# The first matrix product of the second part by one level of Strassen's scheme: seven half-size products instead of eight, 768 tokens at a time

## The chip, the core and the metric

The kernel runs on one core of a Trainium2 chip. The metric is device time in microseconds (us) of one execution, the median of several runs. The engines of the core run side by side, each in its own order: TensorE (PE in the profile, with its weight loads as PEld), VectorE (DVE), ScalarE (ACT), GpSimd (POOL), and SyncE (SP), which here issues DMA transfers. They share the on-chip memory SBUF; PE writes its results into the banks of a second memory, PSUM, from which DVE and ACT read.

## What is computed

```python
def phi(x):
    proj = np.einsum('bhsd,df->bhsf', x, w_phi)
    proj = proj - np.max(np.abs(proj), axis=-1, keepdims=True)
    return np.concatenate([np.exp(proj), np.exp(-proj)], axis=-1)
q_p, k_p = (phi(q), phi(k))
kv = np.einsum('bhsf,bhsd->bhfd', k_p, v)
z = np.sum(k_p, axis=2)
num = np.einsum('bhsf,bhfd->bhsd', q_p, kv)
den = np.einsum('bhsf,bhf->bhs', q_p, z)[..., None] + 1e-06
x = (num / den).transpose(0, 2, 1, 3).reshape(4608, 512)
...
h = x @ w_in
g = h - np.tanh(h)
return (g @ w_out).astype(np.float32)
```

Batch 8, 8 heads, 576 positions, head size 64. The second part takes 4,608 tokens of 512 numbers through w_in (512 x 2048), the function h - tanh(h), and w_out (2048 x 512). The weights of the second part arrive as 64-bit floats.

## The kernel before

**The first part** (`ramp`, `period`, `drain`) runs over 32 units, each a pair of heads of one batch entry, and writes the normalised result of each to `xs` in device memory. Beside it, each period decodes one 128 x 512 tile of w_in or w_out from 64-bit floats (`dec_0` to `dec_3`), and from the fifth period on `split_w` splits one into a high and a low half for the reduced-precision matmul type fp32r: a copy on ACT (`wh`), then the difference `w - wh` on POOL (L96). All of this stands in an order written by hand.

**The second part** runs over nine groups `g` of 512 tokens and, in each, over 16 tiles `f` of 128 columns of w_in: 144 steps. `stage1` (L617) multiplies the tile with the group's tokens: 12 matmuls (four slices of the 512-long contraction, each as high x high, high x low, low x high) of 512 columns into one PSUM bank `ph`. Then ACT and DVE form h - tanh(h): a polynomial for small |h| and the direct difference for the rest, chosen by a mask. ACT makes `y`, `s1`, `s2`, `th`, `mk` (L632 to L640); DVE makes five steps:

```python
nc.vector.scalar_tensor_tensor(s1, s1, PC1, y, ALU.add, ALU.mult)
gs = s2 if g else s1
nc.vector.scalar_tensor_tensor(gs, s2, PC2, s1, ALU.add, ALU.mult)
nc.vector.scalar_tensor_tensor(gs, gs, PA, h, ALU.mult, ALU.mult)
hh = th if g else h
nc.vector.tensor_tensor(hh, h, th, ALU.subtract)
nc.vector.copy_predicated(gs, mk.bitcast(U32), hh)
```

(L641, L643, L644, L646, L647). Here `h` lies in PSUM, so L644 and L646 read one operand from SBUF and one from PSUM; `s1`, `s2`, `y`, `mk`, `th` lie in SBUF, except that in the first group `s2` is a PSUM bank, `ex`, and L646 writes back into PSUM. `split_g` splits the result into `gh` (a copy on ACT, L653) and `gl` (a difference on POOL, L654), and `stage2` (L665) runs 12 matmuls of 512 columns, four token tiles by three, into four PSUM banks `po` that gather over the 16 steps. A step's `stage2` is issued two steps after its `stage1`. While a group runs, `x_load` and `x_split` fetch and split the next group's tokens (L117 on ACT, L118 on DVE), and in the first group the 18 weight tiles that the first part left are split (`late`). The scheduler of the framework orders this part, apart from instructions that `pin` keeps in program order.

Of the kernel before, what the change touches and what calls it, by code (L numbers as in the profile page):

```python
# [32 lines left out]
def tile_linear_attention_moe(  # L33
# [44 lines left out]
    wpa = ctx.enter_context(tc.tile_pool(name="wpa", bufs=1, reuse_waits="tile"))
    xp0 = ctx.enter_context(tc.tile_pool(name="xp0", bufs=1, reuse_waits="tile"))
    wi, wo, wp, xp = {}, {}, [], []  # L80


    def split_w(n, pin=lambda ins: ins):
        d, nm, f = (wi, wo)[n % 2], "io"[n % 2], n // 2
        early = f < AHEAD
        w = d[f]
        wh = (wpa if early else wp[0]).tile([P, DM], F32R, name=f"wh{nm}{f}")
        wl = wpool.tile([P, DM], F32R, tag="w", name=f"wl{nm}{f}")
        if early or nm == "i":
            pin(nc.scalar.copy(wh, w))  # L90
        else:
            pin(nc.vector.tensor_copy(wh, w))
        d[f] = (wh, wl)

        def low():
            pin(nc.gpsimd.tensor_tensor(wl, w, f32(wh), ALU.subtract))  # L96
# [18 lines left out]
    def x_split(xt, c, order=lambda ins: ins):
        xh, xl = (x[:, c, :] for x in xt)
        order(nc.scalar.copy(xh, f32(xl)))  # L117
        order(nc.vector.tensor_tensor(xl, f32(xl), f32(xh), ALU.subtract))  # L118

    with ExitStack() as c1:
        raw = c1.enter_context(tc.tile_pool(name="raw", bufs=2))
        p1 = c1.enter_context(tc.tile_pool(name="p1", bufs=1))
        p2 = c1.enter_context(tc.tile_pool(name="p2", bufs=2))
        dr = ctx.enter_context(tc.tile_pool(name="dr", bufs=3, space=DRAM))
# [94 lines left out]
        def part_of(u, part):  # L223
# [136 lines left out]
        def denom_copy(u):  # L360
            u.dd = p1.tile([P, CH], F32, tag="dd", name=f"dd{u.i}")
# [56 lines left out]

        def ramp():
# [52 lines left out]
        def period(i):  # L472
            a, c, p, r, q, o = (unit(i - n) for n in range(6))
            w = dec[i - 3]
            low = split_w(i - 4) if 4 <= i < 2 * AHEAD + 4 else None
# [43 lines left out]
            if i == NU - 1:  # L519
                for j in range(NCT // 2):  # L520
                    x_split(xt[0], j)
            if i == NU - 2:
                xt[0] = x_tiles(0)
                for j in range(NCT):
                    x_load(0, xt[0], j)
# [13 lines left out]
        def drain():  # L539
# [30 lines left out]
            for j in range(NCT // 2, NCT):  # L570
                x_split(xt[0], j)
# [33 lines left out]
    with ExitStack() as c2:  # L605
        xp.append(c2.enter_context(tc.tile_pool(name="xp", bufs=1, reuse_waits="tile")))
        wp.append(c2.enter_context(tc.tile_pool(name="wp", bufs=1, reuse_waits="tile")))
        gp = c2.enter_context(tc.tile_pool(name="gp", bufs=2, reuse_waits="tile"))
        gm = c2.enter_context(tc.tile_pool(name="gm", bufs=2, reuse_waits="tile"))
        ps_h = c2.enter_context(tc.tile_pool(name="ps_h", bufs=3, reuse_waits="tile", space=PSUM))  # L610
        ps_o = c2.enter_context(tc.tile_pool(name="ps_o", bufs=5, reuse_waits="tile", space=PSUM))

        ex = ps_o.tile([P, DM], F32, tag="o", name="ex")

        def stage1(g, f, xh, xl):  # L617
            n = G
            N = n * P
            ph = ps_h.tile([P, 512], F32, tag="h", name=f"ph{g}_{f}")  # L620
            h = ph[:, 0:N]
            i = 0
            for c in range(NCT):
                for wt, x in ((wi[f][0], xh), (wi[f][0], xl), (wi[f][1], xh)):
                    nc.tensor.matmul(h, wt[:, c * P : (c + 1) * P], x[:, c, 0:N], start=(i == 0), stop=(i == 3 * NCT - 1))  # L625
# [8 lines left out]
            nc.scalar.activation(s1, y, AF.Square, bias=bias_t[:, 0:1])  # L634
            s2 = tmp("s2") if g else ex
            nc.scalar.activation(s2, y, AF.Square, bias=bias_t[:, 1:2])  # L636
            th = tmp("th")
            nc.scalar.activation(th, h, AF.Tanh)
            mk = tmp("o", bufs=3) if (g, f) == steps[-1] else tmp("mk", bufs=1)
            nc.scalar.activation(mk, y, AF.Relu, bias=bias_t[:, 2:3])  # L640
            nc.vector.scalar_tensor_tensor(s1, s1, PC1, y, ALU.add, ALU.mult)  # L641
            gs = s2 if g else s1
            nc.vector.scalar_tensor_tensor(gs, s2, PC2, s1, ALU.add, ALU.mult)  # L643
            nc.vector.scalar_tensor_tensor(gs, gs, PA, h, ALU.mult, ALU.mult)  # L644
            hh = th if g else h
            nc.vector.tensor_tensor(hh, h, th, ALU.subtract)  # L646
            nc.vector.copy_predicated(gs, mk.bitcast(U32), hh)  # L647
            return gs
# [145 lines left out]
```

## Time and profile before

| | us |
|---|---|
| median of 3 runs | 1102.42 (1102.21 to 1102.55) |
| the profiled execution | 1103.19 |
| its span, first to last instruction | 1101.4 |
| first matmul of the second part | 313.15 from the span's start |
| start of the last matmul | 1097.09 |
| DVE busy, 400.20 to 1097.10 | 490.02 of 696.90 |
| ACT busy, the same stretch | 460.96 |
| POOL busy, the same stretch | 170.70 |

The page gives, for each engine, its busy time and its share of the span; then the chain of work that ended last; then groups of instructions by line with their mean duration. A busy share is an average over the two parts, which have different limits, so the second part has its own rows here. The granted TensorE clock is 1.000.

### The profile page before, as it was taken

How to read it: one execution, taken by the hardware profiler on the slowest of the kernel's cores; microseconds unless marked ns; L12 is line 12 of the kernel's file. 1: busy time of each engine (PE TensorE's matmuls, PEld its weight loads, DVE VectorE, ACT ScalarE, POOL GpSimd, SP SyncE). 2: the span in 40 equal slices, each digit the busy share in tenths (PEclk: the TensorE clock that was granted, in tenths of full speed). 3: DMA queues.
4: the chain of work that ended last, by engine and by line, in shares of the span. 5: the costliest groups of instructions: out<-in, count | busy, mean ns of one | idle time of the engine just before them, and what ended most of it. 6: DMA issues, size and time to landing. Idle time of an engine off the chain costs nothing.

```text
span 1101.4 us, 18540 instructions
## 1 busy us (share of the span) xinstructions
PE 1092.3 (99%) x6956; PEld 862.2 (78%) x6956; DVE 838.8 (76%) x1169; ACT 768.9 (70%) x1398; POOL 438.6 (40%) x349
## 2 busy tenths in 40 slices
PE   8999999999999999999999999999999999999998
PEld 6666676766668888888888888888888888888886
DVE  7999999999988777767667667767767676776665
ACT  5888887777877766666667666666666666666665
POOL 4788887666655532322222222222222222222222
PEclk9999999999999999999999999999999999999999
DMA  5677777777630020010011011001002002000001
GB/s 173 185 224 224 221 221 217 216 214 211 210 113 1 1 78 12 33 48 30 1 39 39 1 39 39 1 12 64 1 1 77 1 1 77 1 1 22 17 1 39
DMA packets 51147, 85.46 MB, mean 78 GB/s; under 512 B 13296, under 2 KB 24944, under 8 KB 51056
## 3 DMA queue, kind: packets, MB, share of 16 engines
q1 hardware_dynamic: 36656, 51.89, 14.8%
q10 hardware_dynamic: 14400, 32.38, 9.8%
q8 instruction: 55, 0.90, 0.3%
q14 instruction: 36, 0.29, 0.1%
HBM read 65.08 MB, written 19.02 MB: 76 GB/s over the span
## 4 chain that ended last, share of the span: by engine, by line
PE 98%; ACT 1%; DVE 1%; DMA 0%; POOL 0%; issue 0%; SPq 0%; ACTq 0%; POOLq 0%; DVEq 0%
PE ph L625 35%; PE po L668 12%; PE po L669 12%; PE po L671 12%; PE pc L285 6%; PE po L334 6%; PE pu L348 3%; PE pj L219 3%; PE pa L219 3%; PE ptt L249 2%; PE pc L323 1%; PE pt L219 1%; PE pu L306 1%; PE pu L254 1%; PE pu L315 0%; DMA rb<-rr 0%
## 5 line engine op out<-in xcount | busy, mean ns | idle before, releaser
L654 POOL TENSOR_TENSOR gl<-s,gh 128x512 fp32r<-128x512 f32 x144 | 186.4, 1294 | 551.9 <-ACT gh L653 543.4
L632 ACT ACTIVATE y<-ph 128x512 f32<-128x512 f32 x144 | 86.2, 598 | 252.1 <-PE ph L625 252.1
L641 DVE SCALAR_TENSOR_TENSOR s<-s,y 128x512 f32<-128x512 f32 x144 | 102.2, 710 | 183.8 <-ACT s L634 182.8
L625 PE MATMUL ph<-xh,whi 128*128 128x512 f32 x576 | 224.3, 389 | 0.1
L625 PE MATMUL ph<-xl,whi 128*128 128x512 f32 x576 | 224.1, 389 | 0.0
L625 PE MATMUL ph<-xh,wli 128*128 128x512 f32 x576 | 224.1, 389 | 0.0
L668 PE MATMUL po<-who,gh 128*128 128x512 f32 x572 | 222.6, 389 | 0.0
L669 PE MATMUL po<-wlo,gh 128*128 128x512 f32 x572 | 222.5, 389 | 0.0
L671 PE MATMUL po<-who,gl 128*128 128x512 f32 x572 | 152.9, 389 | 0.0
L647 DVE COPY_PREDICATED s<-mk,th 128x512 f32<-128x512 uint32 x127 | 122.1, 961 | 13.7 <-DVE th L646 0.9
L625 PEld LDWEIGHTS ph<-xh,whi 128*128 128x128 f32 x576 | 108.2, 188 | 23.3 <-DVE s L647 0.5
L625 PEld LDWEIGHTS ph<-xh,wli 128*128 128x128 f32 x576 | 108.2, 188 | 22.5
L625 PEld LDWEIGHTS ph<-xl,whi 128*128 128x128 f32 x576 | 108.0, 188 | 22.3
L668 PEld LDWEIGHTS po<-who,gh 128*128 128x128 f32 x572 | 107.4, 188 | 22.7 <-ACT gh L653 0.4
L669 PEld LDWEIGHTS po<-wlo,gh 128*128 128x128 f32 x572 | 107.4, 188 | 22.2
L671 PEld LDWEIGHTS po<-who,gl 128*128 128x128 f32 x572 | 107.4, 188 | 22.2
L634 ACT ACTIVATE s<-y,bias_t 128x512 f32<-128x512 f32 x144 | 104.4, 725 | 0.4 <-POOL gl L654 0.4
L644 DVE SCALAR_TENSOR_TENSOR s<-s,ph 128x512 f32<-128x512 f32 x144 | 98.9, 687 | 5.2
L640 ACT ACTIVATE mk<-y,bias_t 128x512 f32<-128x512 f32 x143 | 102.8, 719 | 0.0
L643 DVE SCALAR_TENSOR_TENSOR s<-s,s 128x512 f32<-128x512 f32 x128 | 88.5, 692 | 15.0 <-ACT s L636 1.9
L636 ACT ACTIVATE s<-y,bias_t 128x512 f32<-128x512 f32 x128 | 92.4, 722 | 1.6 <-POOL gl L654 1.6
L653 ACT CAST gh<-s 128x512 fp32r<-128x512 f32 x144 | 88.8, 617 | 2.4 <-DVE s L647 2.4
(103 smaller groups left out, 1695.6 us busy)
## 6 DMA issues: line engine op xcount, KB each, us to landing
qk<-in_qkT ACTq DMA_DIRECT2D x27, 576.0 KB
v<-in_v SPq DMA_DIRECT2D x32, 320.0 KB, 4.3
rb<-rr SPq DMA_DIRECT2D x64, 144.0 KB, 2.8
xs<-d SPq DMA_DIRECT2D x32, 288.0 KB, 6.0
out<-o SPq DMA_DIRECT2D x35, 256.0 KB, 2.1
rawo<-in_moe_w_out ACTq DMA_DIRECT2D x16, 512.0 KB, 4.4
rawi<-in_moe_w_in ACTq DMA_DIRECT2D x15, 512.0 KB, 4.3
xl<-xs SPq DMA_DIRECT2D x24, 256.0 KB, 3.4
```

Source lines behind the costliest of these rows:

```text
L625: nc.tensor.matmul(h, wt[:, c * P : (c + 1) * P], x[:, c, 0:N], start=(i == 0), stop=(i == 3 * NCT - 1))
L634: nc.scalar.activation(s1, y, AF.Square, bias=bias_t[:, 0:1])
L636: nc.scalar.activation(s2, y, AF.Square, bias=bias_t[:, 1:2])
L640: nc.scalar.activation(mk, y, AF.Relu, bias=bias_t[:, 2:3])
L641: nc.vector.scalar_tensor_tensor(s1, s1, PC1, y, ALU.add, ALU.mult)
L644: nc.vector.scalar_tensor_tensor(gs, gs, PA, h, ALU.mult, ALU.mult)
L647: nc.vector.copy_predicated(gs, mk.bitcast(U32), hh)
L653: pin(nc.scalar.copy(gh, gs))
L654: pin(nc.gpsimd.tensor_tensor(gl, gs, f32(gh), ALU.subtract))
L668: nc.tensor.matmul(po[t], a, wo[f][0], start=(f == 0), stop=False)
L669: nc.tensor.matmul(po[t], a, wo[f][1], start=False, stop=False)
L671: nc.tensor.matmul(po[t], gl[:, t * P : (t + 1) * P], wo[f][0], start=False, stop=(f == NF - 1))
```

## The change

The second part is rewritten. It takes six blocks `g` of 768 tokens, and in each eight pairs `k` of w_in tiles: 48 frames. In a frame, the 512-long contraction, the 256 columns of w_in and the 768 tokens are each halved. Seven products of half matrices stand for the eight, `product` with six matmuls of 384 columns each. Their operands are sums and differences of the halves. They gather in two PSUM banks, `A` and `B`; ACT copies `A` out (`u1`, `u2`, `u4`) between products, and DVE adds these copies to `B` (`add11`, `add22`, `add21`) into `h`, which now lies in SBUF. X is the upper and Y the lower 768 columns of `h` of a frame. ACT, DVE and POOL work on 768 columns per instruction, with the same five DVE steps (`v_1` to `v_5`). The second product keeps its 36 matmuls of 512 columns per 768 tokens and pair, in four `chunk`s a frame that run one and a half frames late (`LAG = 6`); it has six PSUM banks.

The seven weight operands of a pair, split into high and low, are made by `Prep`: four sums or differences of 128 x 256 on POOL, four ACT copies and four POOL differences. Pairs 0 and 1 are prepared in the first part, pairs 2 to 7 in the first six frames; each is stored to device memory (`ring_store`) and from the second block on loaded again, 1.8 MB a frame (`ring_load`), into a ring of three. Twelve tiles of w_out are split in the same six frames, their copy on DVE and their difference on POOL. The token operands of the next block are made in frames 6 and 7 of a block and frame 0 of the next: four sums (`x_sum`) and five of the seven low halves on POOL, the other two on DVE. For the first block, the four sums lie in the first part, and the low halves on DVE, two in the first part and five in frame 0. The whole program now stands in an order written by hand.

```diff
+    TG = 768
+    HT = TG // 2
     PC = 2 * S
     NCT = DM // P
     NF = DFF // P
     CH = S // 2
+    NFP = NF // 2
+    NG = B * S // TG
...
+    def ring_tile(q):
+        pool = ring_pool[0] if q % 3 < 2 else ring_pool[1]
+        ring[q] = pool.tile([P, 2, 7, 2 * P], F32R, tag=f"r{q % 3}", name=f"wr{q}")
+        return ring[q]
...
+            def sums():
+                self.r = ring_tile(self.k)
+                self.s = [st_any(t, [P, 2 * HT], f"s{self.k}_{t}")[:, 0:DM].rearrange("p (n f) -> p n f", n=2) for t in self.tags]
+                s = self.s
+                sub(s[0][:, 1], w1[:, a], w1[:, b], ALU.add)
+                sub(s[1][:, 0], w0[:, a], w1[:, a], ALU.subtract)
+
+            def sums2():
+                s = self.s
+                sub(s[0][:, 0], s[0][:, 1], w0[:, a], ALU.subtract)
+                sub(s[1][:, 1], w0[:, b], s[0][:, 0], ALU.subtract)
...
+            def hi(n, m, src):
+                nc.scalar.copy(self.r[:, 0, n:m], src())
+
+            def lo(n, m, src):
+                sub(self.r[:, 1, n:m], src(), f32(self.r[:, 0, n:m]), ALU.subtract)
...
+                (lambda: hi(2, 4, lambda: self.s[0]), lambda: lo(2, 4, lambda: self.s[0])),
+                (lambda: hi(4, 6, lambda: self.s[1]), lambda: lo(4, 6, lambda: self.s[1])),
+                (lambda: hi(0, 2, lambda: two(w0)), lambda: lo(0, 2, lambda: two(w0))),
+                (lambda: hi(6, 7, lambda: two(w1[:, b])), lambda: lo(6, 7, lambda: two(w1[:, b]))),
...
-            for c in range(NCT):
-                for wt, x in ((wi[f][0], xh), (wi[f][0], xl), (wi[f][1], xh)):
...
+            for c in range(2):
+                cs = slice(c * P, (c + 1) * P)
+                for a, b in ((0, 0), (0, 1), (1, 0)):
+                    nc.tensor.matmul(
+                        bank[:, 0:HT],
+                        w[:, a, n, cs],
+                        x[:, b, c, :],
...
+        def p1p2(q):
+            A[q] = ps_ab.tile([P, 512], F32, tag="A", name=f"A{q}")
+            Bk[q] = ps_ab.tile([P, 512], F32, tag="B", name=f"B{q}")
+            product(A[q], q, 0, 0, True)
+            product(Bk[q], q, 1, 1, True)
+
+        def p6(q):
+            product(A[q], q, 2, 2, False)
+
+        def p5(q):
+            product(A[q], q, 3, 3, False)
+
+        def p7(q):
+            product(Bk[q], q, 4, 4, True)
+
+        def p4p3(q):
+            product(Bk[q], q, 6, 5, False)
+            product(A[q], q, 5, 6, False)
...
+        def part(q, nm):
+            t = part_t[q, nm] = gp.tile([P, HT], F32, tag="u2" if nm == "u2" else "u1", name=f"{nm}_{q}", bufs=1)
+            nc.scalar.copy(t, A[q][:, 0:HT])
+
+        def add11(q):
+            X[q] = gelu(f"x{q}")
+            nc.vector.tensor_tensor(half(X[q].h, 0), Bk[q][:, 0:HT], part_t.pop((q, "u1")), ALU.add)
+
+        def add22(q):
+            nc.vector.tensor_tensor(half(X[q].h, 1), Bk[q][:, 0:HT], part_t.pop((q, "u4")), ALU.add)
+
+        def add21(q):
+            Y[q] = gelu(f"y{q}")
+            nc.vector.tensor_tensor(half(Y[q].h, 0), Bk.pop(q)[:, 0:HT], part_t.pop((q, "u2")), ALU.add)
+
+        def copy12(q):
+            nc.scalar.copy(half(Y[q].h, 1), A.pop(q)[:, 0:HT])
...
+        def v_1(z):
+            nc.vector.scalar_tensor_tensor(z.s1, z.s1, PC1, z.y, ALU.add, ALU.mult)
+
+        def v_23(z):
+            nc.vector.scalar_tensor_tensor(z.s2, z.s2, PC2, z.s1, ALU.add, ALU.mult)
+            nc.vector.scalar_tensor_tensor(z.s2, z.s2, PA, z.h, ALU.mult, ALU.mult)
+
+        def v_4(z):
+            nc.vector.tensor_tensor(z.th, z.h, z.th, ALU.subtract)
+
+        def v_5(z):
+            nc.vector.copy_predicated(z.s2, z.y.bitcast(U32), z.th)
+
+        def a_gh(z):
+            z.gh = gm.tile([P, 2 * HT], F32R, tag="gh", name=f"gh{z.nm}")
+            z.gl = gm.tile([P, 2 * HT], F32R, tag="gl", name=f"gl{z.nm}")
+            nc.scalar.copy(z.gh, z.s2)
+            nc.gpsimd.tensor_tensor(z.gl, z.s2, f32(z.gh), ALU.subtract)
...
+        def x_sum(g, n):
+            b11, b12, b22, b21 = f32(xop[g][0][:, 1]), xst[g, "b12"], xst[g, "b22"], xst[g, "b21"]
+            o, a, b = (
+                lambda: (st_tile(g, 3, "t1"), b12, b11),
+                lambda: (b12, b22, b12),
+                lambda: (st_tile(g, 4, "t2"), b22, xst[g, "t1"]),
+                lambda: (b21, b21, xst[g, "t2"]),
+            )[n]()
+            nc.gpsimd.tensor_tensor(o, a, b, ALU.subtract)
...
+        def ring_load(q):
+            nc.sync.dma_start(f32(ring_tile(q)).rearrange("p a n f -> p (a n f)"), wd[q % NFP])
...
+            p1p2(q)
+            at("start")
+            part(q, "u1")
+            if yp:
+                a_sq(yp)
+            if xp:
+                v_5(xp)
+                a_gh(xp)
+            at("a1")
+            add11(q)
+            chunk(s)
+            p6(q)
+            part(q, "u2")
+            at("a2")
+            if yp:
+                v_1(yp)
+                a_th(yp)
+                v_23(yp)
+            at("a3")
+            chunk(s + 1)
+            p5(q)
+            if yp:
+                a_mk(yp)
+                v_4(yp)
+                v_5(yp)
+            at("a4")
+            part(q, "u4")
+            p7(q)
+            at("a5")
+            add22(q)
+            if yp:
+                a_gh(yp)
+            at("a6")
+            chunk(s + 2)
+            a_sq(X[q])
+            v_1(X[q])
+            p4p3(q)
+            add21(q)
+            a_th(X[q])
+            copy12(q)
+            chunk(s + 3)
+            a_mk(X[q])
+            v_23(X[q])
+            v_4(X[q])
+            at("end")
...
+                if k == 3:
+                    h["start"].append(lambda: x_loads(nxt))
+                if k == 6:
+                    for n, at in enumerate(("start", "a2", "a4")):
+                        h[at].append(lambda n=n: x_sum(nxt, n))
+                    op("a4", nxt, 0, nc.gpsimd, "a6")
+                if k == 7:
+                    op("a2", nxt, 1, nc.gpsimd, "a2")
+                    op("a4", nxt, 2, nc.gpsimd, "a4")
+                    op("a5", nxt, 3, nc.vector, "a6")
+                    h["a4"].append(lambda: x_sum(nxt, 3))
```

The rows below come from the built programs. First POOL, in the first group or block. Before, over three steps: `gl` is the low half of a step's result, `wli` and `wlo` low halves of weights.

```order
L96 TENSOR_TENSOR wli14_4841<-wi14_4079,whi14_4840 128x512
L654 TENSOR_TENSOR gl0_11_4884<-s10_11_4818,gh0_11_4883 128x512
L96 TENSOR_TENSOR wlo14_4888<-wo14_4142,who14_4887 128x512
L654 TENSOR_TENSOR gl0_12_4931<-s10_12_4871,gh0_12_4930 128x512
L96 TENSOR_TENSOR wli15_4935<-wi15_4222,whi15_4934 128x512
L654 TENSOR_TENSOR gl0_13_4978<-s10_13_4918,gh0_13_4977 128x512
```

In the change, frame 5 of the first block: `s7_3` and `s7_4` are weight sums of pair 7, `wr7` its operands in the ring, `glx4` and `gly4` the low halves of the results X and Y of the frame before, `wlo14` and `wlo15` halves of w_out.

```order
L114 TENSOR_TENSOR s7_3_5032<-wi15_3970 128x256
L115 TENSOR_TENSOR s7_4_5033<-wi14_3718,wi15_3970 128x256
L119 TENSOR_TENSOR s7_3_5032<-s7_3_5032,wi14_3718 128x256
L120 TENSOR_TENSOR s7_4_5033<-wi14_3718,s7_3_5032 128x256
L797 TENSOR_TENSOR glx4_5048<-s2x4_4975,ghx4_5047 128x768
L126 TENSOR_TENSOR wr7_5031<-s7_3_5032,wr7_5031 128x512
L126 TENSOR_TENSOR wr7_5031<-s7_4_5033,wr7_5031 128x512
L797 TENSOR_TENSOR gly4_5107<-s2y4_5042,ghy4_5106 128x768
L126 TENSOR_TENSOR wr7_5031<-wi14_3718,wr7_5031 128x512
L155 TENSOR_TENSOR wlo14_5113<-wo14_4234,who14_5112 128x512
L126 TENSOR_TENSOR wr7_5031<-wi15_3970,wr7_5031 128x256
L155 TENSOR_TENSOR wlo15_5165<-wo15_4260,who15_5164 128x512
```

A frame has twelve instructions where three steps have six, and both new kinds, the sums and `wr`, read two SBUF tensors. Next DVE in a later group. Before, one step; `ph3_4` lies in PSUM, the rest in SBUF:

```order
L641 SCALAR_TENSOR_TENSOR s13_4_6745<-s13_4_6745,y3_4_6743 128x512
L643 SCALAR_TENSOR_TENSOR s23_4_6747<-s23_4_6747,s13_4_6745 128x512
L644 SCALAR_TENSOR_TENSOR s23_4_6747<-s23_4_6747,ph3_4_6730 128x512
L646 TENSOR_TENSOR th3_4_6749<-ph3_4_6730,th3_4_6749 128x512
L647 COPY_PREDICATED s23_4_6747<-mk3_4_6751,th3_4_6749 128x512
```

In the change, one frame of the third block: the five steps of Y of the frame before, the addition `hx20` from bank `B20`, the first step of X, the addition `hy20`, and the other four of X.

```order
L781 SCALAR_TENSOR_TENSOR s1y19_7143<-s1y19_7143,yy19_7142 128x768
L784 SCALAR_TENSOR_TENSOR s2y19_7144<-s2y19_7144,s1y19_7143 128x768
L785 SCALAR_TENSOR_TENSOR s2y19_7144<-s2y19_7144,hy19_7106 128x768
L788 TENSOR_TENSOR thy19_7173<-hy19_7106,thy19_7173 128x768
L791 COPY_PREDICATED s2y19_7144<-yy19_7142,thy19_7173 128x768
L755 TENSOR_TENSOR hx20_7153<-B20_7125,u4_20_7195 128x384
L781 SCALAR_TENSOR_TENSOR s1x20_7218<-s1x20_7218,yx20_7217 128x768
L759 TENSOR_TENSOR hy20_7236<-B20_7125,u2_20_7170 128x384
L784 SCALAR_TENSOR_TENSOR s2x20_7219<-s2x20_7219,s1x20_7218 128x768
L785 SCALAR_TENSOR_TENSOR s2x20_7219<-s2x20_7219,hx20_7153 128x768
L788 TENSOR_TENSOR thx20_7238<-hx20_7153,thx20_7238 128x768
L791 COPY_PREDICATED s2x20_7219<-yx20_7217,thx20_7238 128x768
```

`hy19` and `hx20`, which the third and fourth step read, are now SBUF tensors; the addition from B20 stands behind the five steps of Y. The last place is POOL at a change of blocks, frames 30 and 31, which are frames 6 and 7 of the fourth block (a block's frames are counted from 0):

```order
L866 TENSOR_TENSOR xst4t1_8498<-xst4b12_8102,xo4_0_8100 128x768
L797 TENSOR_TENSOR glx29_8510<-s2x29_8447,ghx29_8509 128x768
L866 TENSOR_TENSOR xst4b12_8102<-xst4b22_8104,xst4b12_8102 128x768
L866 TENSOR_TENSOR xst4t2_8556<-xst4b22_8104,xst4t1_8498 128x768
L797 TENSOR_TENSOR gly29_8569<-s2y29_8504,ghy29_8568 128x768
L850 TENSOR_TENSOR xo4_0_8100<-xo4_0_8100 128x768
L797 TENSOR_TENSOR glx30_8645<-s2x30_8584,ghx30_8644 128x768
L850 TENSOR_TENSOR xo4_1_8667<-xst4b21_8106,xo4_1_8667 128x768
L850 TENSOR_TENSOR xo4_2_8693<-xst4t2_8556,xo4_2_8693 128x768
L866 TENSOR_TENSOR xst4b21_8106<-xst4b21_8106,xst4t2_8556 128x768
L797 TENSOR_TENSOR gly30_8709<-s2y30_8639,ghy30_8708 128x768
```

`xst4` are the sums and `xo4` the low halves of the fifth block's operands, put between the low halves `glx` and `gly` of the results. Before, no such work was on POOL: tokens were split by ACT and DVE.

More of the change, by code (lines that the diff above doesn't have):

```diff
@@ L115, in x_split @@
[L115 to L118, printed above, removed]
+    wd = [dram.tile([P, 14 * 2 * P], F32, name=f"wd{k}") for k in range(NFP)]
+    wi, wo, ring, xop = {}, {}, {}, {}
+    xop_pool, ring_pool, st_pool, xst = [xo], [wr], [stp], {}
+    tiles = [("i", f) for f in range(2 * EARLY_K)]
+    for f in range(NF):
+        tiles += [("o", f), ("i", f + 2 * EARLY_K)] if f + 2 * EARLY_K < NF else [("o", f)]
@@ L519, in period @@
             if i == NU - 1:
[L520 to L525, printed above, removed]
+                x0_split(0)
+            if 17 <= i < 21:
+                x0_load(i - 17)
             num(p)
@@ L665, in stage2 @@
[L665 to L679 removed]
+        st_pool.append(c2.enter_context(tc.tile_pool(name="st2", bufs=1, reuse_waits="tile")))
@@ new lines, in chunk @@
+        def chunk(s):
+            j = s - LAG
+            if not 0 <= j < 4 * NQ:
+                return
+            q, pos = divmod(j, 4)
+            g, k = divmod(q, NFP)
+            z = (X if pos < 2 else Y)[q]
+            n = pos % 2
+            second = pos in (1, 3)
+            f = 2 * k + (pos in (1, 2))
+            if k == 0 and pos < 2:
+                for t in range(3):
+                    acc[g, 3 * second + t] = ps_o.tile([P, DM], F32, tag="o", name=f"po{g}_{3 * second + t}")
+            first, last = k == 0 and pos < 2, k == NFP - 1 and pos >= 2
+            wh, wl = wo[f]
+            tiles = [(acc[g, 3 * second + t], slice(n * HT + t * P, n * HT + (t + 1) * P)) for t in range(3)]
+            for po, ts in tiles:
+                nc.tensor.matmul(po, z.gh[:, ts], wh, start=first, stop=False)
+                nc.tensor.matmul(po, z.gh[:, ts], wl, start=False, stop=False)
+                if last and g == NG - 1:
+                    nc.tensor.matmul(po, z.gl[:, ts], wh, start=False, stop=True)
+            if not (last and g == NG - 1):
+                for po, ts in tiles:
+                    nc.tensor.matmul(po, z.gl[:, ts], wh, start=False, stop=last)
+            if pos == 3:
+                X.pop(q), Y.pop(q)
@@ new lines, in frame, with at @@
+        def frame(q):
+            g, k = divmod(q, NFP)
+            s = 4 * q
+            xp, yp = X.get(q - 1), Y.get(q - 1)
+            h = hooks(g, k)
+            def at(n):
+                for f in h.get(n, ()):
+                    f()
+            p1p2(q)
[43 more added lines that the diff above has]
+            at("end")
@@ L741, in _bits @@
+        for q in range(NQ):
+            frame(q)
+        finish()
 def _bits(u):
```

414 lines of the change are left out of this document (255 added, 159 removed).

## The prediction

> **What bounds the kernel now.** I read the page's busy times and its chain first, then PE's part of the second part by windows and in order of time.
>
> ```profile
> PE 1092.3 (99%) x6956; PEld 862.2 (78%) x6956; DVE 838.8 (76%) x1169; ACT 768.9 (70%) x1398; POOL 438.6 (40%) x349
> PE 98%; ACT 1%; DVE 1%; DMA 0%; POOL 0%; issue 0%; SPq 0%; ACTq 0%; POOLq 0%; DVEq 0%
> 400.20:1097.10 696.90, 696.90 (x3077) 577.23 (x3075) 490.02 (x686) 460.96 (x813) 170.70 (x131) 1.00 0.07 24
> ```
>
> PE is busy in all of the 696.90 us of the window, at full clock, and the chain that ended last is 98% PE. DVE has 490.02 us, ACT 460.96, POOL 170.70. So PE's own matmuls set the time, and removing them pays until another engine is late. What one costs, the order of time shows:
>
> ```profile
> 700.20 0.39 PE L625 MATMUL ph<-xh,whi 128*128 128x512 f32 x1
> 702.92 0.39 PE L668 MATMUL po<-who,gh 128*128 128x512 f32 x1
> 705.64 0.39 PE L625 MATMUL ph<-xh,whi 128*128 128x512 f32 x1
> ```
>
> The first product of a step begins at 700.20, the second at 702.92, the next step at 705.64 (column 1 is the start, column 2 the duration; durations overlap): 24 matmuls in 5.44 us, 0.2267 us each. The 144 steps take 783.4 us.
>
> **What PE saves.** Per 768 tokens and pair of tiles the first product has 42 matmuls of 384 columns for 36 of 512. The trace has no fp32r matmul of 384 columns. Below, its cost is bounded by the weight load before it:
>
> ```profile
> 313.15 0.50 PE L625 MATMUL ph<-xh,whi 128*128 128x512 f32 x1
> 313.49 0.40 PE L625 MATMUL ph<-xl,whi 128*128 128x512 f32 x1
> 313.15 0.19 PEld L625 LDWEIGHTS ph<-xh,whi 128*128 128x128 f32 x1 [0.47 <-issue]
> 313.26 0.19 PEld L625 LDWEIGHTS ph<-xl,whi 128*128 128x128 f32 x1
> ```
>
> After a pause, weights and matmul begin together at 313.15; the matmul lasts 0.50 instead of 0.39, and the next weight load begins 0.11 us later, with the columns. So a load holds a matmul up by 0.11 us and is hidden behind any that streams longer. Above, the cost is bounded by 0.2267, if all of it were fixed. I take the share of the columns, 0.2267 x 384/512 = 0.170, since the loads, 0.11, leave room for it. A frame is then 42 x 0.170 + 36 x 0.2267 = 7.14 + 8.16 = 15.30 us, 48 frames 734.4, a saving of 49.0 us.
>
> The Trainium skill ("TensorE: Matmul & The Clock Gate", section "Back-to-back issue gap") puts the spacing at N/2.4 + 2.5 ns, 162.5 ns for 384 columns, an estimate by that page. For 512 it says 215.8 where the rows show 226.7, so the measurement decides; by the page's figure 2016 products would take 15 us less, and the sum below would be 1111 instead of 1126.
>
> **What DVE and POOL do to each other.** Three places, each engine with the other:
>
> ```profile
> 377.73 1.29 POOL L96 TENSOR_TENSOR wlo<-wo,who 128x512 fp32r<-128x512 f32 x1 [1.08 <-DVE who L92]
> 378.98 1.74 POOL L96 TENSOR_TENSOR wli<-wi,whi 128x512 fp32r<-128x512 f32 x1
> 378.45 1.13 DVE L641 SCALAR_TENSOR_TENSOR s<-s,y 128x512 f32<-128x512 f32 x1 [0.86 <-ACT s L634]
> 379.68 0.69 DVE L643 SCALAR_TENSOR_TENSOR s<-ex,s 128x512 f32<-128x512 f32 x1
> 446.08 1.29 POOL L654 TENSOR_TENSOR gl<-s,gh 128x512 fp32r<-128x512 f32 x1 [2.80 <-ACT gh L653]
> 445.86 0.68 DVE L646 TENSOR_TENSOR th<-ph,th 128x512 f32<-128x512 f32 x1
> 446.64 1.34 DVE L647 COPY_PREDICATED s<-mk,th 128x512 f32<-128x512 uint32 x1
> L644 DVE SCALAR_TENSOR_TENSOR s<-s,ph x144: 676/686/690, 319.5 to 1090.5; 128x512 f32<-128x512 f32 x144
> L646 DVE TENSOR_TENSOR th<-ph,th x128: 682/683/684, 402.3 to 1091.1; 128x512 f32<-128x512 f32 x128
> ```
>
> L641 reads two SBUF tensors. It begins at 378.45 while POOL works until 379.02, and ends at 379.58, 0.56 us after POOL, where it alone would need 0.69. The POOL instruction behind it is recorded at 378.98 and takes 1.74 instead of 1.29: it waits for L641 in turn. L643, with one operand in PSUM, takes 0.69 beside the same POOL instruction. At 446 it is the same: L646 reads PSUM and SBUF and keeps its 0.68 us; L647, all in SBUF, takes 1.34 until 447.98, 0.6 us after gl ended. Over the whole run L644 and L646 never exceed 690 ns (minimum, median, maximum). So a DVE step with two SBUF inputs and a POOL instruction exclude each other, taking turns; one PSUM input frees DVE. The change puts h into SBUF, so all five steps are of the first kind, twice a frame.
>
> Sizes follow from rows of two widths:
>
> ```profile
> L298 POOL TENSOR_TENSOR ss<-ss,kp x32: 1274/1278/1288, 13.1 to 305.8; 128x512 f32<-128x512 f32 x32
> L385 POOL TENSOR_TENSOR d<-d,rb x32: 1407/1414/1910, 43.1 to 463.6; 128x576 f32<-128x576 f32 x32
> L238 DVE TENSOR_TENSOR t<-pa,m 128x1024 f32<-128x1024 f32 x31 | 38.0, 1225 | 3.2
> L238 DVE TENSOR_TENSOR t<-pa,m 128x512 f32<-128x512 f32 x2 | 1.4, 692 | 0.1
> ```
>
> POOL: (1414 - 1278)/64 = 2.1 ns a column, so 1.82 us for 768 and 0.73 for 256; 512 stays 1.29. DVE: (1225 - 692)/512 = 1.04 ns a column. Between two POOL instructions a 512-column step adds 379.02 to 380.72, less 1.29, = 0.41 us; a 768-column one 0.41 + 0.27 = 0.68.
>
> **Regular frame.** POOL has two gl, 3.6 us, and DVE ten steps, 6.8: together 10.4 of 15.3, so PE keeps the pace. I walked one to see the slack. Products P1 and P2 end 2.0 us after the frame's start, P7 (bank B) 9.2, and P4, which adds to B, may start at 11.2, if add22 has read B. add22 stands behind the five steps of Y, whose first waits for ACT's squares:
>
> ```profile
> 447.94 0.59 ACT L638 ACTIVATE th<-ph 128x512 f32<-128x512 f32 x1
> 448.41 0.72 ACT L634 ACTIVATE s<-y,bias_t 128x512 f32<-128x512 f32 x1
> 449.02 0.72 ACT L636 ACTIVATE s<-y,bias_t 128x512 f32<-128x512 f32 x1
> ```
>
> They follow each other by 0.47 to 0.61 us at 512 columns, by 0.7 to 0.9 at 768 by the share of columns, so after u1 (1.4) and two squares the first step starts near 3.1. Steps of 0.9 us, one of them held by gl until 6.8, put the fifth's end at 9.5 and add22's at 10.0. PE has 1.2 us to spare. ACT, with six such operations for each of X and Y and four copies of 384, has about 11 of 15.3 us.
>
> **Change of blocks** (frames 6, 7 and the next 0). POOL gets nine more 768-column instructions, DVE two more steps. By loads: POOL 15 x 1.82 = 27.3, DVE 32 x 0.68 = 21.8, together 49.1 against 45.9, 3.2 us over. By walking, taking turns: in frame 6 the steps end 4.1, 5.0, (gl 6.8) 7.6, (sum 9.4) 10.1, (sum 11.9) 12.7, and add22 13.2 holds P4 by 1.9 us. Frame 7 begins with DVE a microsecond later, with three more POOL instructions in the same place: 4.4. Frame 0 with two: 2.4. So 3.2 to 8.7 per change, of which there are five; I take 6, nearer the walk, since the order in each queue is fixed.
>
> **First block.** In frames 1 to 5 POOL has four sums (2.9), low halves of weights (3 x 1.29 + 0.73 + 2 x 1.29 = 7.2) and two gl (3.6), 13.7 us, and DVE's ten steps between them 6.8: 20.5 us against 15.3 of PE (11.2 in frame 1, which has two chunks only). Frame 0 has 10.1 + 7 x 0.68 = 14.9, and begins about 5 us after PE, since its scratch is held until DVE splits two operands, behind the last decode:
>
> ```profile
> 315.92 0.69 DVE L183 SCALAR_TENSOR_TENSOR wo<-rawo,pt 128x512 uint32<-128x512 uint32 x1
> ```
>
> POOL is through at 313.2 + 5 + 14.9 + 5 x 20.5 = 435.6; PE, whose add22 stands halfway in POOL's frame, leaves frame 5 some 6 us earlier, at 429.6. PE's own work would end at 313.2 + 7.1 + 11.2 + 4 x 15.3 = 392.7. Loss 37 us, with those 6 us pushed into the first change of blocks, 5 of which I count there.
>
> **What lies beside.** Loading 1.84 MB a frame is 120 GB/s, where the first part moves
>
> ```profile
> GB/s 173 185 224 224 221 221 217 216 214 211 210 113 1 1 78 12 33 48 30 1 39 39 1 39 39 1 12 64 1 1 77 1 1 77 1 1 22 17 1 39
> ```
>
> up to 224, and a load has a frame and more to land: nothing. SP's queue carries stores and loads in order, and a store of weights waits for POOL at most until that weight's own frame. In the first part the prepared sums take the place of weight splits of the same size on POOL and ACT: nothing, give or take 1 us. At the end, six chunks cover the last Y: nothing.
>
> **The sum.** The profiled execution took 1103.2 us, 1.8 above its span and 0.8 above the median. 1103.2 - 49 + 37 + 5 + 5 x 6 = 1126 us.
>
> **Rivals.** (1) PE stays the bound. For it: POOL is busy a quarter of the window now, DVE 70%, and POOL's instructions may fall where DVE waits for ACT. Then frame 0's fill costs about 10 us, and 1103.2 - 49 + 10 = 1064. It decides if POOL's first-block frame is under 8.5 us instead of 13.7. (2) Only the first block is late, since changes of blocks stay under PE's slack of 1.2 us a frame: 1103.2 - 49 + 37 = 1091. (3) A matmul of 384 columns costs nearly what one of 512 does: 17.7 us a frame, +65, and the first block still 20 late: 1188. Against it stands the load's 0.11 us.
>
> **How the numbers follow.** The exclusive turns are seen in every such meeting, so the forecast has 0.58 (own range 1105 to 1150), rival 1 0.19, rival 2 0.15, rival 3 0.08. The range of 1060 to 1152 takes in rivals 1 and 2, and leaves out rival 3 and the ends. A difference of 0.2%, 2 us, is about what a measurement can tell. Faster: 0.19 + 0.15 = 0.34; the forecast's lower edge gives 0.03 to the same; slower 0.63.
>
> **What would show it.** PE rows of 384 columns 0.17 us apart; frames of some 20 us until about 430; DVE steps of 768 columns with a mean far over 0.96 us, ending after POOL instructions; PE idle ahead of P4, released by DVE's addition, in frames 6, 7 and 0 and not in 2 to 5 of later blocks. A first block near 80 us would make the prediction wrong, and so would 384-column matmuls 0.2 us apart.

## The result, and the profile after

| | us |
|---|---|
| before, median of 4 runs | 1102.49 (1102.21 to 1103.02) |
| after, median of 4 runs | 1174.97 (1172.76 to 1176.13) |
| ratio, with its 95% interval | 1.0654 (1.0636 to 1.0673) |
| the profiled execution after; its span | 1174.16; 1172.4 |

The change makes the kernel 6.5% slower. The prediction had the sign, but 1175 lies outside its range of 1060 to 1152. The page of the kernel after, with busy times, the chain that ended last, and the granted clock in 40 slices:

```profile
PE 1096.5 (94%) x7244; PEld 909.2 (78%) x7244; DVE 1005.7 (86%) x1062; ACT 847.3 (72%) x1321; POOL 636.9 (54%) x397
PE 54%; DVE 27%; ACT 8%; issue 4%; POOL 3%; DMA 2%; POOLq 0%; DVEq 0%; SPq 0%; ACTq 0%
PEclk9999999999979888999999999999999999999999
```

PE is down from 99% of the span to 94%, and DVE has entered the chain with 27%. What PE waited for, the three longest lists (us in total, times, longest wait):

```profile
PE B L708 <- DVE hx L755: 45.7, 21, 4.9
PE po L825 <- POOL glx L797: 6.9, 6, 2.6
PE B L708 <- POOL xo L850: 6.8, 5, 1.5
```

L755 is `add22`: product P4 may write bank B only when it has been read. 13.1 of its 45.7 us lie in frames 0 to 5 of the first block, the rest at the changes of blocks. Three stretches of 20 us show the places (busy time with number of instructions in the order PE, PEld, DVE, ACT, POOL; granted clock, DMA share, GB/s), and then, in order of time, the same place of two successive regular frames:

```profile
334.00:354.00 20.00, 14.15 (x51) 12.43 (x52) 15.96 (x13) 11.50 (x18) 18.91 (x12) 0.74 0.19 81
534.00:554.00 20.00, 20.00 (x101) 17.86 (x100) 17.31 (x17) 15.20 (x22) 8.21 (x4) 1.00 0.55 202
714.00:734.00 20.00, 17.52 (x80) 15.54 (x79) 17.45 (x14) 12.98 (x18) 12.86 (x6) 0.91 0.28 98
```
```profile
540.03 0.39 PE L819 MATMUL po<-who,ghx 128*128 128x512 f32 x1
555.74 0.39 PE L819 MATMUL po<-who,ghx 128*128 128x512 f32 x1
```

The first stretch lies in the first block: POOL is busy 18.9 of 20 us and PE 14.2, at a mean clock of 0.74. The second lies in regular frames: PE is never idle, at full clock, yet a frame takes 15.71 us and not 15.30. The third lies at a change of blocks. Frame 22 (frame 6 of the third block) begins at 715.02. Its first three POOL instructions, then DVE's beside and behind them (start, duration):

```profile
720.16 2.66 POOL L797 TENSOR_TENSOR glx<-s2x,ghx 128x768 fp32r<-128x768 f32 x1 [5.31 <-ACT ghx L796]
722.78 2.56 POOL L866 TENSOR_TENSOR xst3b<-xst3b,xst3b 128x768 f32<-128x768 f32 x1
725.29 2.53 POOL L866 TENSOR_TENSOR xst3t<-xst3b,xst3t 128x768 f32<-128x768 f32 x1
720.14 0.96 DVE L784 SCALAR_TENSOR_TENSOR s2y<-s2y,s1y 128x768 f32<-128x768 f32 x1
721.13 2.50 DVE L785 SCALAR_TENSOR_TENSOR s2y<-s2y,hy 128x768 f32<-128x768 f32 x1
723.56 2.59 DVE L788 TENSOR_TENSOR thy<-hy,thy 128x768 f32<-128x768 f32 x1
726.25 2.44 DVE L791 COPY_PREDICATED s2y<-yy,thy 128x768 f32<-128x768 uint32 x1
728.59 0.54 DVE L755 TENSOR_TENSOR hx<-B,u 128x384 f32<-128x384 f32 x1
```

They take turns: each DVE step ends 0.8 us after a POOL instruction (723.63 after 722.82, 726.15 after 725.34, 728.69 after 727.82), and each lasts 2.5 us instead of 0.96. `add22` ends at 729.13, 14.1 us into the frame. PE in the same place:

```profile
715.02 1.23 PE L708 MATMUL A<-xo,wr 128*128 128x384 f32 x6
729.18 1.75 PE L708 MATMUL B<-xo,wr 128*128 128x384 f32 x6 [2.48 <-DVE hx L755]
730.73 2.12 PE L708 MATMUL A<-xo,wr 128*128 128x384 f32 x6
732.65 0.63 PE L819 MATMUL po<-who,ghx 128*128 128x512 f32 x1
733.08 0.48 PE L820 MATMUL po<-wlo,ghx 128*128 128x512 f32 x1
735.02 1.21 PE L708 MATMUL A<-xo,wr 128*128 128x384 f32 x6
736.07 1.20 PE L708 MATMUL B<-xo,wr 128*128 128x384 f32 x6
```

Behind the wait, six matmuls take 1.92 us (730.73 to 732.65), 0.32 each, where six later ones take 1.05 (735.02 to 736.07), 0.175 each: after its idle time PE ran at about half speed for 3 us. The granted clock says the same: 0.50 from 729.83 to 733.24 (last section).

**Where the time went.** The frames, from first product to first product, give the whole difference from the sum of the prediction:

| term | predicted | measured | how measured |
|---|---|---|---|
| PE's saving | -49.0 | -29.3 | 783.4 - 48 x 15.71 |
| first block | +37 | +42.4 | its frames 0 to 5 take 124.1; at PE's own pace 81.7 (frame 0 without chunks, frame 1 with two) |
| five changes of blocks | +35 | +56.9 | frames 6, 7 and the next 0 and 1: 13.8, 11.7, 10.5, 10.5, 10.4 over regular frames |
| begin of the second part | 0 | +1.0 | 314.2 for 313.15 |
| sum with 1103.2 | 1126 | 1174.2 | profiled: 1174.16 |

### The profile page after: what moved, and what is told of

Same layout as the page of the kernel before. It is cut to its first block, busy times and chain, and to the rows that moved or that the text cites. A ratio compares the mean times of both kernels' runs of the same rounds, so it can differ in the third digit from the quotient of the medians.

```text
span 1172.4 us, 19032 instructions
## 1 busy us (share of the span) xinstructions
PE 1096.5 (94%) x7244; PEld 909.2 (78%) x7244; DVE 1005.7 (86%) x1062; ACT 847.3 (72%) x1321; POOL 636.9 (54%) x397
## 4 chain that ended last, share of the span: by engine, by line
PE 54%; DVE 27%; ACT 8%; issue 4%; POOL 3%; DMA 2%; POOLq 0%; DVEq 0%; SPq 0%; ACTq 0%
PE A L708 9%; PE B L708 7%; PE pc L322 6%; PE po L819 5%; PE po L820 5%; PE po L825 5%; DVE thy L788 5%; PE po L371 5%; DVE s2y L785 4%; DVE s2y L784 3%; PE pu L385 3%; DVE s2y L791 3%; PE pj L256 2%; DVE s1x L781 2%; PE pa L256 2%
## 5 line engine op out<-in xcount | busy, mean ns | idle before, releaser
L797 POOL TENSOR_TENSOR glx<-s2x,ghx 128x768 fp32r<-128x768 f32 x48 | 103.1, 2149 | 290.8 <-ACT ghx L796 282.7
L708 PE MATMUL A<-xo,wr 128*128 128x384 f32 x1152 | 245.5, 350 | 5.3 <-ACT u L748 4.0
L708 PE MATMUL B<-xo,wr 128*128 128x384 f32 x864 | 185.5, 350 | 53.1 <-DVE hx L755 45.7
L708 PEld LDWEIGHTS A<-xo,wr 128*128 128x128 f32 x1152 | 215.6, 196 | 20.1 <-ACT u L748 5.0
L708 PEld LDWEIGHTS B<-xo,wr 128*128 128x128 f32 x864 | 157.1, 195 | 68.4 <-DVE hx L755 57.9
L819 PE MATMUL po<-who,ghx 128*128 128x512 f32 x288 | 117.4, 407 | 0.0
L820 PE MATMUL po<-wlo,ghx 128*128 128x512 f32 x288 | 116.0, 403 | 0.0
L820 PE MATMUL po<-wlo,ghy 128*128 128x512 f32 x288 | 113.4, 394 | 0.0
L819 PE MATMUL po<-who,ghy 128*128 128x512 f32 x288 | 113.3, 393 | 0.0
L785 DVE SCALAR_TENSOR_TENSOR s2y<-s2y,hy 128x768 f32<-128x768 f32 x48 | 106.5, 2218 | 1.7
```

The costliest lines, as they stand in the source:

```text
L708: nc.tensor.matmul(bank[:, 0:HT], w[:, a, n, cs], x[:, b, c, :], start=start and i == 0, stop=i == 5, skip_group_check=not start,)
L785: nc.vector.scalar_tensor_tensor(z.s2, z.s2, PA, z.h, ALU.mult, ALU.mult)
L797: nc.gpsimd.tensor_tensor(z.gl, z.s2, f32(z.gh), ALU.subtract)
L819: nc.tensor.matmul(po, z.gh[:, ts], wh, start=first, stop=False)
L820: nc.tensor.matmul(po, z.gh[:, ts], wl, start=False, stop=False)
```

## The experiments

Twelve kernels, each run once with a profile, beside a run of the kernel before on the same chip (1102.5 to 1103.2 in all three groups). Differences from the kernel after are taken from its median. Three theories stood at the start: the turns that POOL and DVE take cost the time (1), the work on POOL is too much or too late in itself (2), the loading of weights slows PE and the other engines (3).

**E1 and E2: POOL as busy, without reading.** E1 replaces each sum and low half of the token operands on POOL by two writes of a constant, E2 does so with the sums and low halves of weights in the first block, by three each. The operands then hold constants, and the rest of the program works on these. The sums in E1:

```diff
-            nc.gpsimd.tensor_tensor(o, a, b, ALU.subtract)
+            for _ in range(2):
+                nc.gpsimd.memset(o, 0.01)
```

> At each change of blocks the nine POOL instructions that make the next block's token sums and low halves are replaced by two POOL memsets each on the same tile: about as long in all (0.8 us each by the memset rows of 512 columns, 1.6 for 1.8), but reading nothing from SBUF. The sums and low halves are left out, so the output is not the reference's. Theory 1 (DVE steps with two SBUF inputs and POOL instructions that read SBUF take turns, and the chain v_1 to v_5, add22, P4 is held): frames 6, 7 and 0 of the blocks fall from 20.0, 17.9 and 19.3 us to 15.7 to 16.5, so 40 to 50 us less in all, about 1128. Theory 2 (POOL has simply too many instructions there and delivers late): the same frames, within 1 us, about 1170. Theory 3 (the loads of weights, 1.8 MB a frame, slow the engines): no change.

> In the first block POOL's sums of weights and low halves of weights of pairs 2 to 7 and of the twelve late w_out tiles are replaced by three memsets each on the same tile (POOL about as long, nothing read); they are left out of the computation. Theory 1: the frames 2 to 5 of the first block fall from 19.0 to 23.1 us to 16 to 17, the block from 165 to about 140, about 1150 in all. Theory 2 (POOL alone is too full, 13.7 us of a frame plus what it waits for): frames of 19 us or more stay, 1170 or more. Theory 3: no change in this block, since it has no loads.

E1 took 1121.42 us, 53.5 less; E2 1151.41, 23.6 less. PE's waits for `add22` and the writes themselves, two rows of E1 and then two of E2 (where lines are counted six higher):

```profile
PE B L708 <- DVE hx L755: 13.7, 7, 2.3
L852 POOL MEMSET xo<- 128x768 f32 x50 | 36.5, 741 | 1.4
```
```profile
PE B L714 <- DVE hx L761: 37.4, 21, 4.6
L113 POOL MEMSET wr<- 128x512 f32 x54 | 28.9, 543 | 2.1
```

Two writes take 1.48 us, somewhat less than the 1.82 of the difference they replace; three of E2 take 1.63, more than its 1.29. POOL had about as much to do, and PE's wait went with the reading: frames 6, 7 and the next 0, 17.9 to 23.3 us before the edit, take 15.7 to 16.4, and frames 2 to 5 of the first block fall from 21.4 in the mean to 17.2. A write also waits for no operands, which could make POOL earlier; but in frame 22 of the kernel after, POOL had no gap between its three instructions. And the DVE steps themselves show it. Frame 22 in E1, the writes and the two DVE steps beside them:

```profile
698.89 1.54 POOL L871 MEMSET xst3b<- 128x768 f32 x2
700.37 1.54 POOL L871 MEMSET xst3t<- 128x768 f32 x2
699.69 0.95 DVE L788 TENSOR_TENSOR thy<-hy,thy 128x768 f32<-128x768 f32 x1
700.74 1.07 DVE L791 COPY_PREDICATED s2y<-yy,thy 128x768 f32<-128x768 uint32 x1
```

The same two steps took 2.59 and 2.44 us beside POOL's sums. Over E1, E2 and E7, 185 DVE instructions of 768 columns ran beside such writes alone, and none took over 1.10 us, the longest beside an idle POOL; in the kernel after, those beside a reading POOL instruction take up to 2.61. Theory 1 holds in both places.

**E7: both at once**, the edits of E1 and E2 in one kernel.

> The edits of the first two runs together: POOL writes only, in the first block and at the changes of blocks; weight sums, late low halves and token sums are left out of the computation. The two gains should add, 1175 - 54 - 24 = 1097: the time of this scheme with only the low halves of the results left to take turns. Under theory 1 that is the most that any moving of POOL's work could bring.

```profile
PE B L714 <- DVE hx L761: 6.0, 6, 1.4
```

1097.36 us: 1175.0 - 53.5 - 23.6 = 1097.9, so the two gains add. With this much work left undone the kernel is 0.5% ahead of the one before: about what the scheme would take if POOL's extra work cost DVE nothing. It isn't shown to be a limit, since frames 2 to 5 of the first block still take 17.2 us here, beside a POOL that is kept busy with writes.

**E3: no weight loads.** From the second block on, the ring gives prepared weights that are there already, so pairs are multiplied with other pairs' weights.

```diff
-                h["start"].append(lambda: ring_load(q + 2))
+                h["start"].append(lambda: ring.update({q + 2: ring[(6, 7, 5)[(q + 2) % 3]]}))
```

> From the second block on no weights are loaded: each frame uses one of the three weight sets left in the ring by the first block, so the first product of blocks 1 to 5 has the wrong weights. Theory 1: no change, 1170 to 1176, and regular frames stay at 15.7 us. Theory 3 (loads): regular frames fall to the 15.3 us forecast, or the changes of blocks by some us each; 1140 to 1155.

```profile
534.00:554.00 20.00, 20.00 (x101) 17.95 (x100) 17.40 (x18) 14.81 (x21) 8.21 (x4) 1.00 0.10 31
```

1175.75 us, no change: in the same stretch 31 GB/s instead of 202, and the same 101 matmuls. Regular frames keep their 15.71 us. Theory 3 falls, and the matmuls, slower than forecast, have another cause.

**E5: the kernel before with 384 columns.** The kernel before with groups of 384 tokens for 512: first products of 384 columns beside second ones of 512, without Strassen's scheme.

```diff
-    G = 4
+    G = 3
```

> The kernel before with groups of 384 tokens for 512 (G = 3), so that its first product has matmuls of 384 columns beside the second's of 512, with no other part of the change; same result as the reference. It tells what a 384-column matmul costs. By the share of columns: 170 ns apart, and 227 for 512 columns. By what the changed kernel's regular frames show (175.8 and 231.2): 174 to 176, and 231. If the two widths side by side cost nothing by themselves, the 512-column ones stay at 226.7.

PE in order of time, one step and the end of its first product:

```profile
702.79 0.33 PE L625 MATMUL ph<-xh,whi 128*128 128x384 f32 x1
703.86 0.33 PE L625 MATMUL ph<-xh,whi 128*128 128x384 f32 x1
704.90 0.39 PE L668 MATMUL po<-who,gh 128*128 128x512 f32 x1
706.98 0.33 PE L625 MATMUL ph<-xh,whi 128*128 128x384 f32 x1
```

1123.46 us, 21 more than before. Twelve matmuls of 384 columns take 2.11 us (702.79 to 704.90), 0.1758 each; the nine of 512 behind them 2.08, 0.231 each, where the kernel before has 0.2267. With 42 x 0.1758 + 36 x 0.231 = 15.70, that is the regular frame of the kernel after. So the 0.41 us that a frame has over 15.30 come with the two widths side by side, not with the scheme. (E5 also has nine matmuls of 512 columns in a row where the kernel before has twelve; the two aren't separated.) The last six of the twelve take 1.04 us, 0.1733 each, so even there 384 columns cost more than three quarters of 0.2267.

**E4, E6 and E8: the work moved to DVE.** E4 moves the sums and most low halves of the token operands to DVE, into places later in the frames. In it operand 1 of the later blocks is split from the fourth sum instead of the raw quarter (a difference in what is computed, not in the amount, though its expectation says that the result is the reference's). E6 does the move in an order that computes the reference, with all sums and low halves on DVE. E8 adds the weight sums and late low halves of the first block.

```diff
-            nc.gpsimd.tensor_tensor(o, a, b, ALU.subtract)
+            nc.vector.tensor_tensor(o, a, b, ALU.subtract)
...
-                    op("a4", nxt, 0, nc.gpsimd, "a6")
+                    op("a4", nxt, 0, nc.vector, "a6")
```

> Same result as the reference. At a change of blocks the four sums go to DVE, behind add22 in frames 4 and 5 (in the first block frame 6), where DVE waits for ACT; low halves 0 to 3 go to DVE too, and only those of operands 4 and 5 stay on POOL, in frame 0. Theory 1: the losses of a change fall from about 10.5 us to 2 to 4, five times, so 30 to 42 us less: 1133 to 1145. Theory 2: similar, since POOL is relieved; so this run tells whether the loss can be repaired, not by which theory. Theory 3: no change.

> All nine POOL instructions of a change of blocks go to DVE, most of them behind add22, where DVE waits for ACT; the second sum of the first token half is made only when its raw values have been used. Same result as the reference. Theory 1: a change of blocks loses 1 to 3 us instead of 10.5, so 1125 to 1138 in all; POOL's 768-column instruction holds the other engine for 1.8 us, DVE's for 0.7 to 0.8. Theory 2 (POOL's own lateness): about the same. If DVE's time were the limit, moving work to it would gain nothing: 1165 or more.

> As the run with all token work on DVE, and in the first block the weight sums of pairs 3 to 7 and the low halves of the late w_out tiles go to DVE too; POOL keeps the low halves of the weights in the ring and of the results. Same result as the reference. Theory 1: by loads POOL 8.2 us and DVE 10 steps and 8 smaller ones, some 8.7 us of port time, 17 us a frame for 20.5, so frames of 18 to 19 us in place of 21.4, 10 to 15 us less than the run with the token work moved alone; 1112 to 1125, still above 1102.

E4 took 1146.24 us, E6 1149.85, E8 1152.04, all above what was expected. PE's waits of E6, and a stretch of the first block in E8:

```profile
PE B L708 <- DVE hx L755: 24.1, 13, 2.4
PE po L825 <- POOL glx L797: 6.5, 6, 1.5
PE A L708 <- DVE xo L850: 5.5, 6, 1.2
```
```profile
334.00:354.00 20.00, 14.05 (x57) 11.82 (x57) 19.62 (x21) 12.26 (x20) 9.77 (x7) 0.83 0.22 93
```

E6 gets back 25 of the 53.5 us that E1 did: behind the first block, frames 6 and 7 are regular again, but frame 0 of a block takes 21 to 22 us, since DVE now makes the operands that PE waits for (L850) and its steps are late behind them. E8 was expected to gain another 10 to 15 and gained nothing: in the first block POOL is down from 18.9 to 9.8 of 20 us, and DVE is up from 16.0 to 19.6. The work that fills the frame has changed its engine. A version faster than the kernel before did not come of it.

**E9 to E12: where h lies.** The kernel before, with `gl` made twice (E9) or three times (E11) by the same instruction, and the same with `y`, in SBUF, in place of `h`, in PSUM, in L644 and L646 of all groups but the first (E10, E12; the activation is then another function).

```diff
-            nc.vector.scalar_tensor_tensor(gs, gs, PA, h, ALU.mult, ALU.mult)
+            hs = y if g else h
+            nc.vector.scalar_tensor_tensor(gs, gs, PA, hs, ALU.mult, ALU.mult)
             hh = th if g else h
-            nc.vector.tensor_tensor(hh, h, th, ALU.subtract)
+            nc.vector.tensor_tensor(hh, hs, th, ALU.subtract)
```

> The kernel before, with the instruction that makes gl on POOL issued twice (the same result): POOL then has 2.6 us of a step's 5.44. Theory (where h lies decides): the two DVE steps that read h from PSUM keep 0.69 us, only the other three wait for POOL; DVE and POOL together have 2.6 + 3 x 0.69 = 4.7 us that exclude each other, so PE keeps the pace: 1102 to 1106 us. Rival (POOL's amount alone decides, wherever h lies): the time is the same as in the run beside it whose h is replaced by an SBUF tensor, and L644 and L646 grow as much in both.

> As the run beside it, and in all blocks but the first the two DVE steps that read h from PSUM read y in SBUF instead (the activation is then another function; nothing else changes). Theory: all five DVE steps exclude POOL, 2.6 + 5 x 0.69 = 6.0 us in a step of 5.44, at the least 2.6 + 5 x 0.41 = 4.7 if part of each step overlaps: L644 and L646 grow from 0.69 to 0.9 us or more in the mean, the time rises by 0 to 75 us, I take 20. Rival: no difference from the run beside it.

> The kernel before, with gl made three times on POOL: 3.9 us of a step's 5.44. Theory: L644 and L646 still keep 0.69 us; 3.9 + 3 x 0.41 to 0.69 = 5.1 to 5.9 us of exclusion in 5.44, so 1102 to 1170 us. Rival: the same time as the run beside it with h replaced, and L644 and L646 grown as much.

> As the run beside it, with y in SBUF read for h in the two DVE steps of all blocks but the first (another function of the same size). Theory: 3.9 + 5 x 0.41 to 0.69 = 5.9 to 7.3 us of exclusion in a step of 5.44: slower than the run beside it by 50 us or more (128 steps by at least 0.4), with PE waiting for what follows from DVE and POOL, and its clock lowered behind the longer waits. Rival: no difference.

The times are 1120.07, 1138.29, 1280.01 and 1320.69 us. The two steps (minimum, median, maximum in ns) with `h` in PSUM, in E9 and then in E11:

```profile
L644 DVE SCALAR_TENSOR_TENSOR s<-s,ph x144: 676/686/690, 319.1 to 1105.0; 128x512 f32<-128x512 f32 x144
L646 DVE TENSOR_TENSOR th<-ph,th x128: 681/683/687, 404.6 to 1105.6; 128x512 f32<-128x512 f32 x128
```
```profile
L644 DVE SCALAR_TENSOR_TENSOR s<-s,ph x144: 672/687/690, 319.4 to 1263.9; 128x512 f32<-128x512 f32 x144
L646 DVE TENSOR_TENSOR th<-ph,th x128: 677/684/686, 425.6 to 1264.5; 128x512 f32<-128x512 f32 x128
```

The same two with `y`, a line number higher, in E10 and then in E12:

```profile
L645 DVE SCALAR_TENSOR_TENSOR s<-s,y x128: 683/1661/1781, 403.9 to 1122.9; 128x512 f32<-128x512 f32 x128
L647 DVE TENSOR_TENSOR th<-y,th x128: 631/678/1910, 401.8 to 1117.5; 128x512 f32<-128x512 f32 x128
```
```profile
L645 DVE SCALAR_TENSOR_TENSOR s<-s,y x128: 683/1659/1827, 425.6 to 1302.8; 128x512 f32<-128x512 f32 x128
L647 DVE TENSOR_TENSOR th<-y,th x128: 625/1740/1814, 421.5 to 1295.5; 128x512 f32<-128x512 f32 x128
```

With one operand in PSUM no instance exceeds 0.69 us, however busy POOL is. With both in SBUF the median of the first is 1.66 us, and the second reaches 1.74 in the median in E12 (in E10, with one POOL instruction fewer, it is mostly free, 0.68, but up to 1.91). The place of the operand decides, as the theory of the turns says; it costs 18 us beside two `gl` and 41 beside three (expected: about 20, and 50 or more). E9's and E11's own size was missed: 17 and 177 us above the kernel before, where 0 to 4 and 0 to 68 were expected. PE waits for `gl` for 6.9 us in E9 and 118 in E11, its longest lists, and runs slower behind these waits; so the longer way from DVE over POOL to PE is late, which the count of excluding time leaves out.

## Why the prediction had the sign and missed the size

- **The mechanism was right.** DVE steps with two SBUF inputs and POOL instructions that read SBUF take turns, one PSUM input frees DVE (E9 to E12); this makes the first block and the changes of blocks late (E1, E2, E7), and most of the wait is `add22` ahead of P4, as walked: 32.5 of some 40 us at the changes, 13.1 of 24.8 in the first block. Loads cost nothing (E3), and regular frames have no wait.
- **"What PE saves" was mis-sized by 19.7 us**, the 48 x 0.41. The prediction scaled 0.2267 by the columns to 0.170 and left 512 columns as they were. E5 has 0.1758 and 0.231 without the scheme. Of the loss, 42 x 48 x 3.3 ns = 7 us is what a 384-column matmul costs at its best here (0.1733) over 0.170, the rest that both widths are slower when they alternate. Why alternation costs this isn't settled; the loading of weights from device memory is excluded (E3). The Trainium skill ("TensorE: Matmul & The Clock Gate", section "Back-to-back issue gap") gives N/2.4 + 2.5 ns for isolated matmuls, by which 384 columns would take 162.5 ns, an estimate by that page; the measured 173.3 and 175.8 are further from it than from the share of the columns, 170.
- **"Change of blocks" was mis-sized by 22 us**, and in it the price of PE's clock was missing altogether. The walk gave 8.7 us a change, and the prediction took 6, towards the count of loads: 5 x 2.7 = 13.5 us too little. In frame 22, PE idles for 2.5 us, and the slow stretch behind costs 1.64: twelve product matmuls in 3.47 us instead of 2.11 (729.18 to 732.65), and two slow ones of 512. Such stretches, at a granted clock of 0.50, cost 11.2 us in the five changes. Without them the changes lose 45.7 us, less the 5 of the first block 8.1 each, near the walk's 8.7. That the sum fits is in part luck. Without the clock, frames 22, 23 and 24 lose 2.6, 2.2 and 3.6 us, where the walk had 1.9, 4.4 and 2.4. In frame 22, the first step of Y began 4.1 us into the frame (719.08) instead of 3.1, behind DVE's work on X.
- **"First block" was mis-sized by 5 us**: frames 2 to 5 take 19.0 to 23.1 us, in the mean 21.4 against 20.5. Of the 42.4 us, PE waits for 24.8 and loses about 14 at half clock. How much of the 14 only fills time in which POOL, busy for 18.9 of 20 us, was late anyway isn't shown.
- **"The tail" and "the first part" at nothing** held within 1 us: the second part begins at 314.2.
- **Rival 1**, PE stays the bound, is refuted by 45.7 us of waits for L755. Rival 2, only the first block late, by the five changes with 56.9 us. Rival 3, 384 columns cost like 512, by 0.1758 to 0.231; but of the 114 us between it and the forecast's saving, 19.7 were real.

## What to carry to other kernels

Fewer matmuls pay only as long as the engines that feed them keep pace: before an operand moves from PSUM to SBUF, count the DVE steps that then have two SBUF inputs and the POOL instructions beside them that read SBUF as one queue, and walk that queue in its order; where walk and count differed (8.7 and 3.2 us a change), the walk was nearer here. A matmul's cost didn't scale with its columns here (0.1758 us for 384, not 0.170), so a width that the trace doesn't have is to be measured in the same mix. And a wait of PE costs more than its own length, if the clock falls behind it: 2.5 us of idle time cost another 1.6.

## What the runs showed of the hardware that was not expected

- Behind some of its waits PE ran at half speed for about 3 us: 0.32 us for 384 columns, 0.427 for 512 (732.65 to 733.08). The length of the wait alone doesn't decide. The wait at 612.33 has the length of the one at 748.62, 1.93 us, and only the first was followed by a slow stretch:

```profile
612.33 1.32 PE L708 MATMUL B<-xo,wr 128*128 128x384 f32 x6 [1.93 <-DVE hx L755]
748.62 1.33 PE L708 MATMUL B<-xo,wr 128*128 128x384 f32 x6 [1.93 <-DVE hx L755]
610.36:613.77 3.41, 1.48 (x9) 1.45 (x9) 3.41 (x3) 1.87 (x3) 3.41 (x3) 1.00 0.01 2
613.77:617.18 3.41, 3.41 (x11) 3.02 (x10) 3.26 (x3) 2.84 (x5) 2.23 (x1) 0.50 0.27 59
729.83:733.24 3.41, 3.41 (x12) 3.31 (x11) 1.94 (x3) 3.32 (x5) 3.41 (x2) 0.50 0.00 0
746.89:750.30 3.41, 1.68 (x9) 1.68 (x10) 3.41 (x3) 2.10 (x3) 3.41 (x3) 1.00 0.00 0
750.30:753.71 3.41, 3.41 (x19) 3.01 (x18) 3.26 (x4) 2.82 (x5) 2.02 (x1) 1.00 0.48 126
```

- In this trace the granted clock of the second part is 0.50 or 1.00, and until the last frame it is 0.50 for 3.41 us or 6.83 at a time. The begins lie on one grid: from 613.77 to 729.83 are 34 x 3.413 us, from there to 866.36 and on to 1002.89 40 each. PE was idle for 1.93 us of the span of this grid before 613.77, and for 1.73 of the one before 750.30, which was followed by full clock. So how a wait falls on the grid decides with its length; where the edge lies isn't settled.
- Matmuls of 512 columns are 2% slower (0.231 for 0.2267 us) where matmuls of 384 stand between them, in the kernel after and in E5.
- A POOL instruction that only writes SBUF leaves DVE steps with two SBUF inputs at their 0.95 to 1.07 us (E1), where one that reads makes them 2.4 to 2.6.
- From 0.2267 for 512 columns and 0.1733 for 384, an fp32r matmul here costs 0.417 ns a column (53.4 ns over 128 columns) and about 13 ns besides, an estimate from two widths.
